# A fused attention and maxout kernel on one core: another table of order, engines and slots for the same 1542 nodes

## The chip, the cores and the metric

The kernel runs on one core of one Trainium2 chip, as one launch. The metric is device time in microseconds, taken as the median of several executions. The profile is of one further execution, and all durations here come from its trace.

## The reference

For each of 8 batches and 8 heads (576 tokens, head size 64) there is a linear attention with a feature map, and behind it one feed-forward layer that takes the larger of three products:

```python
def phi(x):                                   # w_phi: 64 x 128
    proj = np.einsum('bhsd,df->bhsf', x, w_phi)
    proj = proj - np.max(np.abs(proj), axis=-1, keepdims=True)
    return np.concatenate([np.exp(proj), np.exp(-proj)], axis=-1)
q_p, k_p = phi(q), phi(k)
kv = np.einsum('bhsf,bhsd->bhfd', k_p, v);  z = np.sum(k_p, axis=2)
attn = np.einsum('bhsf,bhfd->bhsd', q_p, kv) / (np.einsum('bhsf,bhf->bhs', q_p, z)[..., None] + 1e-06)
x = attn.transpose(0, 2, 1, 3).reshape(4608, 512)
h = np.maximum(np.maximum(x @ w1, x @ w2), x @ w3)    # 512 x 768 each
out = h @ w_out                                       # 768 x 512
```

## The kernel before, in words

**Units and chunks.** The attention is cut into 16 units of four heads (two units make one batch), the feed-forward layer into 9 chunks of 512 tokens: the first 512 tokens of each batch, and one chunk of the last 64 tokens of all batches. The program first writes down 1542 nodes in a list. A node is a small piece of work of one engine: its instructions, the nodes it depends on, the buffers it uses, and a guess of its cost. Nothing is issued while they are written down.

**The nodes of a unit u**, by the names that the code gives them (lines are those of the profile of before):

- loads: `L` (main part of q and of k, 512 tokens of each head), `Lt` (q or k of the last 64 tokens, called tails here, for two units at once, as two transfers), `Lv` and `Lw` (the same of v). Units 0 to 3 load the main parts of q and k on POOL's queue with a cast to bf16 (L474); unit 0's k comes in two halves on SP's queue (L461) and is cast by `C` (L466). Everything else is loaded from SP's queue (L373, L378). `C` on POOL (L504) casts tails, and for units 4 to 15 the main parts too.
- `T` transposes q and k: for units 0 to 3 on PE (L517) with `Tc` copying out (L520), from unit 4 on as a DMA transpose on SP (L530).
- `G` projects q and k (L557, L552); `r` takes the largest magnitude (DVE, L576); `ek` the exponentials of k (ACT, L570); `E` the factors that undo the shift on the side of v (ACT, L613).
- `va` multiplies v with these factors on POOL (L618 for the main part, L633 for the tails); `vd` copies the factors beside them (L628, L642).
- `K` multiplies features of k with v (PE, L682, L685), 18 matmuls a node, two nodes a unit; `kv` copies out (L689).
- `M` projects q with its shift (L653 to L657), `eq` is its exponential (L665), `N` the numerator and denominator (L703), `x` the division (L709, L710), `X` the transposition back (PE L723 for units 0 to 5, a DMA transpose later) and `Xc` its copy (L726). From unit 4 on `mT` and `V` send the shift of q through a small DMA (L588, L592).

**The nodes of the weights**: `W` loads one weight matrix with a cast on POOL's queue (L434, 768 KB of bf16 each); `wt`, `we`, `wm`, `mo` form w1 @ w_out (L843 to L861); `wd` forms w2 - w1 and w3 - w1 on POOL and DVE (L831). **The nodes of a chunk**: `up` and `up2` (PE, L756), `t1` and `h` (L764, L766, L762), `down` (L784 and L789), `osb` (L797), `store` (L804).

**What sets the order.** A table, `PLAN`, written out as a string (line 91 of before). Each word has the node's number, a letter for its engine (T for PE, D for DVE, A for ACT, G for POOL, S for SP), the slots of the buffers whose first user it is, and a start in microseconds as the search that made the table believed it. `plan` reads the table:

```python
n.eng, n.start = {"T": "PE", "D": "DVE", "A": "ACT", "G": "POOL", "S": "SP"}[what[at]], float(start)
n.end = n.start + n.costs[n.eng] + LATENCY[n.eng]
for b in n.bufs:
    if b.index is None:
        b.index = int(next(slots), 36)
```

`fill` then puts products of a constant tile, whose result nobody reads (`idler`, L889), into the stretches in which the table leaves PE without work, and sorts everything by its start; the kernel issues the nodes in that order. Engines take their own instructions strictly in that order. So the starts matter in two ways only: as an order on each engine, and as the places of idlers. What an instruction waits for at run time comes from its data and its buffers.

**Three kinds of waits that the steps need.** The raw tiles of q tails and k tails have one buffer each, so the tails of units 2 and 3 can't be loaded before POOL has cast those of units 0 and 1. The bf16 tile of q and k (`qk_bf`) has three slots, so unit 3's loads wait until unit 0's transposes are done. SP issues one transfer after another: one that has to wait holds back all behind it.

Of the kernel before, what the change touches and what calls it, by code (L numbers as in the profile page):

```python
# [105 lines left out]
191D@36.4 200D@37.0 243G@28.8 247G@29.6 132G@29.9 129G@30.9 134G@31.9 128G@32.2 133G@33.2 152T61@35.0 154T2@35.7
155A@36.5 203A@36.9 153A@37.3 1161T5@36.3 1145G@34.2 1162A@37.8 188A@38.3 196D@37.7 204D@38.3 78T20@37.6 68T0@37.9
79D0@38.6 69A@38.8 194A@39.3 187D@39.2 158T61@38.3 156T5@38.7 159D1@39.8 157D0@40.4 162T4@39.0 160T2@39.4 163D1@41.1
161D0@41.7 202A@39.8 206A0@40.1 184A@40.4 173S@33.2 221T11@39.9 224T7@40.4 212T6@40.6 174S@33.8 316S0@37.3 318S0@39.7
253T3@41.0 254D1@42.3 317S@42.0 387S@43.4 249T5@41.3 82T4@41.8 222A@40.9 70A@41.4 84T0@42.3 1163T2@42.6 80T3@43.9  # L110
83D1@42.5 85D0@43.1 225A@41.8 226A@42.3 223A@42.7 213A@43.2 214A@43.8 250D@43.8 245D@44.4 164T7@44.2 88T4@44.5
315S@46.1 89A@45.1 81D1@44.5 1147G@37.5 1164D@45.1 215T1@44.8 388S@47.8 86T0@45.3 166T6@45.6 165D@45.7 87D@46.2
216A@45.7 167A@46.2 255T10532411@45.9 246S@49.5 218T7@46.5 273T0@47.0 1149G@39.6 1148G@41.7 257A@46.9 275A@47.5
217A@47.8 274A@48.3 256A@48.6 1152D@46.7 262D@47.3 220A@49.1 219A@49.8 209A0@50.2 1175T6@47.2 1176D1@48.3 1173T2@48.1
1179T1@48.9 1171T6@49.8 210G0@44.7 208G@45.9 211G@47.8 207G@48.3 227T71@50.7 1174A@50.4 1172A@50.9 321G1@51.8
322G@53.0 229T2@51.3 230A@52.2 259D@49.3 1180D@50.1 251T3@51.9 1189T1@52.5 277D@50.7 258D@51.0 276D@51.6 1151D@52.0
252D@52.7 1150D@53.3 228A@52.6 264T6502@53.5 272D@54.3 1183T7@54.1 392G2@54.1 391G@54.3 390G@55.3 393G@56.3
1177T3@55.1 267D@54.9 271D@55.5 270A@55.1 269A@55.7 1178A@56.2 1184D@56.1 235T60@55.9 236D0@56.8 268D@57.4 263D@58.0
290T00@56.3 296T2@56.7 291A@57.0 284T3@57.0 286A@57.6 297A@58.1 298A@58.6 1190D@58.6 1191T7@57.4 265A@59.0 285A@59.4
292A@59.9 278A1@60.4 1192D@59.2 1169T6@58.3 323S0@54.2 1187T2@59.1 260A@60.7 266A@61.2 261A@61.6 281A1@62.1 1188D@60.3  # L120
237T1@60.0 231T7@60.3 293T3@60.6 233T0@61.1 295A@62.3 294A@62.9 1181T2@61.4 1193T5@62.3 238D1@60.9 232D0@61.5
1170D@62.1 234D1@62.7 458S0@57.1 459S@57.7 461S0@60.3 324T01174600@63.1 283A1@63.4 1182D@63.3 327D@64.0 342T0@63.7
1167G@56.6 280G@60.8 325A@64.0 282G@62.7 279G@63.9 1185T3@64.0 287T2@64.9 329A@64.5 288A@65.6 346D@64.6 1186D@65.2
394S2@61.6 1197T1@65.3 460S@64.5 299T30@66.2 300A@67.1 289A@67.5 1194T@66.8 328D@65.8 332D@66.4 345D@67.0 344A@68.0
319S0@65.1 343A@68.5 326A@68.8 331D@67.3 305T31@68.1 303T4@68.5 301T2@68.8 302A@69.6 330A@70.0 306D0@68.7 304D1@69.3
1195D0@69.9 1198T@69.4 1199A1@70.9 532G0@65.8 528S@66.7 320S@68.4 527S@71.1 464G1@66.1 465G@71.8 333T0734@70.7
337D@71.5 336D@72.1 340D@72.7 466S1@73.1 334A@72.3 339A@72.8 241T2@71.3 242A@73.3 309T6@71.7 307T5@72.0 308D0@73.3
310D1@74.0 1205T1@72.3 1206T@73.2 395T10032511@74.5 335A@73.9 1201T7@75.1 347T6@76.0 341D@74.6 350A0@75.3 338A@75.6
353G0@75.7 533G@76.0 531G@76.3 351G@77.3 530G@79.1 352G@80.1 401A@76.1 400A@76.7 402D@75.3 398D@75.9 313T2@76.1
311T4@76.4 239T0@76.7 348D0@76.5 1202T@77.0 240A@77.3 1207A2@77.9 1203A3@78.6 314D@76.7 403D@77.4 312D@78.0 397A@79.2  # L130
404T6205@78.3 413T4@78.9 407D@79.1 411D@79.7 399D@80.4 416D@81.0 410A@79.7 406A@80.2 355A0@80.6 409A@80.9 412D@81.5
1211T1@79.2 408D@82.2 1217T7@80.1 1215T6@80.9 1227T0@81.8 1212A0@81.4 396A@81.9 405A@82.9 1216D@82.8 418T1@82.7
1213T5@82.7 349S@76.9 389S@77.6 596S0@80.3 600S1@81.5 356T31@83.6 1209T6@83.8 1228D@83.5 419D1@84.1 417D@84.3
1214D@84.7 1210D@85.3 1218D@85.9 421A1@84.8 1208S@82.8 595S@83.4 420S@84.5 357A@85.1 358A@85.7 365T2@84.7 368T0@84.9
1223T1@85.0 424A1@86.2 354G@82.0 665S0@85.2 597S@85.8 1196S@86.4 370A@86.4 414A@86.7 1219T5@85.9 359T6@86.8 369A@87.0
360A@87.4 371T31@87.0 373T7@87.6 362T0@88.2 372D@87.9 1224D@88.3 1220D@88.9 669G2@84.8 664S@87.0 367A@87.9 361A@88.3
366A@88.8 1225T3@88.5 377T61@89.3 415A@89.3 1226D@89.6 436T10@89.7 425G1@85.2 1221T2@89.9 374D@90.2 378D0@90.6
364A@89.7 363A@90.3 375T5@90.7 381T4@91.1 376D1@91.3 382D0@91.9 439T3@91.4 379T7@91.5 430T0@91.8 1231T6@92.0
427T5@92.9 380D1@92.6 1222D@93.2 1229T4@93.1 1230D@94.3 1232D@94.9 433T7@94.0 438A@90.8 437A@91.4 441A@91.9 431A@92.3
383T1@94.2 428A@93.4 429A@94.0 422G@86.5 423G@88.4 426G@90.2 442T20@94.5 440A@94.5 434A@94.8 435A@95.5 432A@96.0  # L140
444T5@95.2 443D@95.5 445D@96.0 385T3@95.8 384D@96.4 386A@96.5 467T01462700@96.1 475D@96.9 471D@97.5 472A@97.7
# [4 lines left out]
491A0@104.6 477A@104.9 478A@105.5 670G@95.5 601G1@95.8 602G@96.9 668G@98.0 1238T@104.3 493A0@106.0 535T10510311@105.6
456T4@106.2 454T2@106.6 537A@106.4 457A@106.9 455A@107.6 603S2@98.1 1204S@102.8 540A@108.2 492S@105.0 1241T6@106.9
1239D1@105.8 538D@106.5 542D@107.1 544T7540@107.8 551D@108.6 547D@109.3 543D@109.9 548D@110.5 553T2@108.4 549A@108.7
550A@109.3 555A@109.8 536A@110.2 554A@110.7 541A@111.0 556D@111.1 552D@111.5 557D@112.1 539D@112.4 1242T@108.7
# [771 lines left out]
```

## Time and profile before

| | us |
|---|---|
| median of three timed executions | 297.06 (296.61 to 297.08) |
| span of the profiled execution, first to last instruction | 295.1 |
| PE busy in the span | 281.6 |
| DVE, ACT, POOL busy | 214.3, 196.3, 138.1 |
| idlers on PE | 37 products, 12.2 busy |
| mean granted PE clock | 0.998 |

The profiled execution is one of its own; its record is the span, and the timed median is 1.96 us longer than that span, because a timed execution also has what lies ahead of the first and behind the last instruction. Matmuls are pipelined: a 128x512 one is shown as busy for 379 ns, while the next starts 216 ns after it. So shares of busy time on PE overstate its work, and the distance between starts is the better measure.

### The profile page before, as it was taken

To read this page: it belongs to the slowest core of one execution; us is meant where nothing else is said; L and a number is where in the kernel's file an instruction comes from. 1 tells how busy PE (TensorE), PEld (TensorE's weight loads), DVE (VectorE), ACT (ScalarE), POOL (GpSimd) and SP (SyncE) were. 2 spreads that over 40 slices of the span, in tenths; PEclk is the share of its full clock that TensorE was granted. 3 is DMA by queue.
4 is the path that set the end of the run, shared out by engine and by line. 5 is a ranking of instruction groups with operands and counts; after the bars stand their busy time and mean duration, and the time that the engine had idled before them with its cause. 6 is when DMAs were issued, how large, how long until landed. Compare 5 with 4: busy or idle time off the path is not lost.

```text
span 295.1 us, 7535 instructions
## 1 busy us (share of the span) xinstructions
PE 281.6 (95%) x2973; PEld 161.5 (55%) x3015; DVE 214.3 (73%) x453; ACT 196.3 (67%) x457; POOL 138.1 (47%) x172
## 2 busy tenths in 40 slices
PE   8699999999999999999999999999999999999994
PEld 3356676556556556556556555655555564444442
DVE  5793798987878988888879776889697365061541
ACT  2499888587878599979879788867954870300300
POOL 4487995672773464943982369009072500000000
PEclk9999999999999999999999999999999999999999
DMA  6999998799379979997979779935392034300306
GB/s 134 190 196 224 229 221 286 167 234 226 99 182 328 209 203 318 230 230 167 285 165 189 220 204 244 189 102 117 90 209 64 2 83 116 142 2 0 142 8 134
DMA packets 87879, 50.02 MB, mean 170 GB/s; under 512 B 56100, under 2 KB 83364, under 8 KB 87844
## 3 DMA queue, kind: packets, MB, share of 16 engines
q1 hardware_dynamic: 81684, 44.50, 61.2%
q0 software_dynamic: 6080, 4.98, 11.0%
q8 instruction: 23, 0.38, 0.5%
q14 instruction: 12, 0.10, 0.1%
q10 hardware_dynamic: 80, 0.07, 0.1%
HBM read 34.67 MB, written 9.44 MB: 149 GB/s over the span
## 4 chain that ended last, share of the span: by engine, by line
PE 79%; DVE 9%; ACT 4%; POOL 3%; DMA 2%; issue 2%; POOLq 0%; ACTq 0%; DVEq 0%
PE ups L756 27%; PE ops L789 15%; PE ops L784 11%; PE psn L703 6%; PE kvps L682 5%; PE psq L557 4%; PE psm L653 4%; DVE mk L576 2%; DMA qk_bf<-in_q_dram 2%; ACT Ek L570 2%; DVE mqp L576 2%; DVE x_sb L710 1%; POOL vab L618 1%; PE pxT L723 1%; DVE w_bf L831 1%
## 5 line engine op out<-in xcount | busy, mean ns | idle before, releaser
L756 PE MATMUL ups<-xT,w_bf 128*128 128x512 bf16 x412 | 100.4, 379 | 2.2 <-DVE mqp L576 0.8
L665 ACT ACTIVATE Eq<-psm 128x512 bf16<-128x512 f32 (+1 forms) x160 | 79.6, 579 | 8.8 <-PE psm L653 7.3
L570 ACT ACTIVATE Ek<-psk 128x512 bf16<-128x512 f32 x128 | 70.8, 607 | 16.1 <-DVE mk L576 8.7
L618 POOL TENSOR_TENSOR vab<-v_raw,em 128x1024 bf16<-128x1024 f32 (+1 forms) x36 | 61.6, 1715 | 21.2 <-ACT em L613 20.1
L756 PEld LDWEIGHTS <-w_bf 128*128 128x128 bf16 x432 | 40.7, 98 | 45.3 <-issue 1.0
L576 DVE TENSOR_REDUCE mqp<-psq 128x4 bf16<-128x512 f32 (+1 forms) x80 | 47.7, 629 | 7.5 <-PE psk L557 4.4
L789 PE MATMUL ops<-wout_bf,hT 128*128 128x512 bf16 (+1 forms) x211 | 49.5, 373 | 0.6 <-issue 0.2
L762 DVE TENSOR_TENSOR hT<-hT,ups 128x512 bf16<-128x512 bf16 x54 | 36.0, 683 | 17.4 <-PE ups L756 9.1
L576 DVE TENSOR_REDUCE mk<-psk 128x4 f32<-128x512 f32 x64 | 42.2, 680 | 1.1 <-PE psk L557 0.7
L710 DVE TENSOR_TENSOR x_sb<-psn,rden 128x320 bf16<-128x320 f32 x64 | 31.5, 492 | 2.2
L789 PEld LDWEIGHTS <-hT 128*128 128x128 bf16 x222 | 21.1, 98 | 21.7
L797 ACT COPY osb<-ops 128x512 f32<-128x512 f32 (+1 forms) x20 | 11.5, 581 | 31.3 <-PE ops L789 23.6
L764 ACT ACTIVATE hT<-ups 128x512 bf16<-128x512 f32 x27 | 16.4, 617 | 21.5 <-PE ups L756 21.5
L703 PEld LDWEIGHTS <-Eq 128*128 128x128 bf16 x640 | 24.6, 97 | 6.8
L703 PE MATMUL psn<-kv_sb,Eq 128*128 128x65 bf16 x640 | 26.1, 194 | 0.1
L633 POOL TENSOR_TENSOR vtl<-v_raw,em 64x256 bf16<-64x256 f32 x32 | 19.7, 615 | 13.2 <-ACT em L613 10.2
L766 DVE TENSOR_SCALAR hT<-ups 128x512 bf16<-128x512 f32 x27 | 18.1, 683 | 10.6 <-PE ups L756 10.6
L784 PE MATMUL ops<-xT 128*128 128x512 bf16 x89 | 24.1, 379 | 0.4
L682 PEld LDWEIGHTS <-Ek 128*128 128x128 bf16 x512 | 21.6, 98 | 4.5 <-DVE mqp L576 0.5
L682 PE MATMUL kvps<-vab,Ek 128*128 128x65 bf16 x512 | 22.8, 194 | 0.5 <-DVE mqp L576 0.2
L504 POOL CAST qk_bf<-q_raw 128x128 bf16<-128x128 f32 (+2 forms) x22 | 16.8, 773 | 11.6 <-DMA q_raw<-in_q_dram 11.3
L797 DVE COPY osb<-ops 128x512 f32<-128x512 f32 (+1 forms) x17 | 11.4, 671 | 13.7 <-PE ops L789 13.6
(80 smaller groups left out, 333.5 us busy)
## 6 DMA issues: line engine op xcount, KB each, us to landing
v_raw<-in_v_dram SPq DMA_DIRECT2D x16, 512.0 KB, 6.8
out_dram<-osb SPq DMA_DIRECT2D x32, 256.0 KB, 2.9
k_raw<-in_k_dram SPq DMA_DIRECT2D x12, 512.0 KB, 5.6
q_raw<-in_q_dram SPq DMA_DIRECT2D x12, 512.0 KB
w_bf<-in_moe_w_dram POOLq DMA_DIRECT2D x3, 768.0 KB, 8.3
k_raw<-in_k_dram SPq DMA_DIRECT2D x16, 64.0 KB, 4.5
q_raw<-in_q_dram SPq DMA_DIRECT2D x16, 64.0 KB, 6.4
v_raw<-in_v_dram SPq DMA_DIRECT2D x16, 64.0 KB, 4.3
```

The lines of the kernel that those rows point to most:

```text
L570: nc.scalar.activation(Ek[s]()[:, t0:t0 + n, :], of(1), EXP, scale=1.0 - 2.0 * s)
L576: nc.vector.tensor_reduce((mq, mk)[c]()[:, t0:t0 + n], of(c), AXX, ALU.max, apply_absolute_value=True)
L618: (nc.vector if n_.eng == "DVE" else nc.gpsimd).tensor_tensor(vab()[:, g, t0:t1, 0:D], raw_part(u, 2, t0, t1), em()[:, g, t0:t1].unsqueeze ...
L665: nc.scalar.activation(Eqb()[s][:, cols], psm()[:, 0:n * P], EXP, scale=1.0 - 2.0 * s)
L682: nc.tensor.matmul(kvps()[:, ab, g, :], lhsT=Ek[g]()[:, t, :], rhs=vab()[:, g, t, :], start=(g + ab + c == 0), stop=False)
L703: nc.tensor.matmul(psn()[:, c, :], lhsT=Eqb()[g][:, t0:t0 + P], rhs=kv()[:, pr, ab, g, :], start=(g == 0), stop=(g == 1))
L710: nc.vector.tensor_tensor(x_sb()[:, pr, :, ab, :], psn()[:, :, 0:D], rden().to_broadcast([P, 5, D]), ALU.mult)
L756: nc.tensor.matmul(ups(), lhsT=w_bf[i + 1][:, ct, j * P:(j + 1) * P], rhs=tokens_of(ct), start=(ct == 0), stop=(ct == CT - 1))
L762: nc.vector.tensor_tensor(hT()[:, j, :], hT()[:, j, :], ups(), ALU.max)
L784: nc.tensor.matmul(ops_()[:, 0:width], lhsT=tile_of(ct, tt), rhs=line_w[c_i > MOVE][:, ct, cols], start=(ct == 0), stop=False)
L789: nc.tensor.matmul(ops_()[:, 0:width], lhsT=hT()[:, j, tt * P:(tt + 1) * P], rhs=wout_bf[:, j, cols], start=False, stop=(j == JT - 1))
L797: copy_on[n_.eng](part()[:, 0:width], ops_()[:, 0:width])
```

## The change

Only the table changes: the 156 lines of `PLAN` become 154. No instruction, cost, dependency or buffer count is touched. Of the 1542 nodes, 88 go to another engine (of the first evacuations of the maxout, `t1`, 16 go from DVE to ACT and 6 back; of `osb` 10 each way; of `vd` 17, of `kv` 13, of `Xc` 6, of `mT` 5, and a few more), 547 get other slots, and the order on every engine is another from the first microseconds on. The words now stand in the order of their starts. PE has 24 idlers instead of 37. Line numbers after the table are lower by 2.

The head of the table, and the last line of each:

```diff
 PLAN = """
-9S0@0.7 4S@1.3 11S@2.5 13S@3.1 8S0@4.4 15S0@5.6 14S@6.9 6G0@0.5 0G@1.4 1G@2.1 7G@2.6 90G1@3.4 17G@9.3 91G@9.6 12A@6.8
-2D0@0.5 3D@0.8 10D@5.3 18T1@5.9 5D@5.7 19D0@6.7 29T002300@7.5 94G@10.4 95G@10.7 20T4@7.8 24T56@8.3 32D@8.0 21D@8.7
-33D@9.3 27D@9.9 16G@10.9 1143G@11.1 34T71@9.4 39T24@9.7 22T5@11.3 38D@10.5 28D@11.1 30A@10.0 31A@10.7 40A@11.2
...
-1532S@292.7 1536S@293.9
+9S0@0.4 6G0@0.4 2D0@0.4 3D@0.8 4S@1.0 7G@1.2 0G@2.1 11S@2.2 1G@2.8 8S0@2.8 91G1@3.3 10A@3.5 13S@4.1 90G@4.2 5D@4.4
+18T1@4.4 170G2@5.0 19D0@5.1 12A@5.3 15S0@5.3 168G@5.8 24T002300@5.9 92D@5.9 29T45@6.1 27D@6.4 25A@6.4 20T6@6.4
+1143G@6.7 30A@6.8 28D@7.0 16G@7.5 21D@7.6 26A@7.8 17G@7.8 95G@8.1 32D@8.2 22T7@8.2 31A@8.2 94G@8.3 34T12@8.4 244G0@8.6
+169S0@8.7 100T6@8.8 23D@8.8 35A@8.9 39T34@9.0 37D@9.1 44T7@9.3 243G@9.4 41A@9.5 42D@9.7 36A@10.0 171S0@10.0 47D@10.3
+1146G@10.3 40A@10.4 33D@10.6 62T10@10.8 45A@10.9 1144G@11.1 59T3@11.2 14S@11.2 38D@11.2 49A0@11.4 63A@11.6 68T5@11.6
...
+1537T0@282.9 1475A2@283.2 1538T@283.4 1476S@283.9 1539D0@284.3 1540S@284.8 1541A@284.8
 """
```

**What stands where in the first part**, read from the built programs' order on each queue:

| queue | before | after |
|---|---|---|
| SP | k halves and w_phi, k tails, q tails, v tails of units 0 and 1, `Lv` of unit 0 (node 14), k tails and q tails of units 2 and 3 (171, 169), `Lv` of unit 1 (93) | k halves and w_phi, q tails, k tails, v tails of units 0 and 1, q tails and k tails of units 2 and 3 (169, 171), then `Lv` of unit 0 (14) and of unit 1 (93) |
| POOL | q of unit 0, first half (6), the identity, second half (7), q of unit 1, casts of tails, k of unit 1 between them, W of w1 and w_out, `va` of unit 0, loads of unit 2 and k of unit 3, rest of `va` of unit 0, w2, casts of the tails of units 2 and 3, `va` of unit 1, w3, `wd` | both halves of q of unit 0, the identity, k and q of unit 1, k and q of unit 2, w1, the four casts of tails of units 0 and 1 (16, 17, 95, 94), k and q of unit 3, w_out, w2, w3, the four casts of tails of units 2 and 3 (247, 175, 176, 248), then all of `va` of unit 0 (57, 55, 54, 50, 51) and of unit 1 |
| PE | transposes of unit 0's main part, all four `G` of that part, then the transposes of unit 0's tails (22) | transposes of unit 0's main part, two `G`, then the transposes of unit 0's tails (22), then the other two `G` |
| PE, ahead of the first `K` of unit 0 | all `T` and `G` of units 0 and 1, 9 `M`, 3 `wt`, 35 idlers | the same `T` and `G`, all `T` of unit 2, one of unit 3, 6 `M`, 3 `wt`, 24 idlers |

The last store of before is issued on SP in two pieces; after, it is one piece on SP and one on ACT.

More of the change, by code (lines that the diff above doesn't have):

```diff
@@ L146 @@
[L146 to L149, printed above, removed]
-1251T4@110.0 1257T7@110.9 1269T3@111.8 735S0@105.7 734S@107.0 802S@107.6 546A@111.5 1243A3@112.0 545A@112.6
@@ new lines @@
+101D1@11.8 1145G@11.9 43D@12.0 46A@12.1 98T2@12.2 69A@12.4 96T6@12.6 48D@12.6 60A@12.9 247G@12.9 99D@13.0
+122T11411@13.2 175G@13.2 61A@13.6 97D@13.6 117T72@13.8 93S@13.9 70A@14.0 65T3@14.2 125D@14.2 53A@14.5 121D@14.6
+176G@14.8 64A@14.8 248G@15.0 177T6@15.1 120D@15.2 57G0@15.2 118A@15.3 179T5@15.5 126D@15.8 66A@15.8 107T17@16.1
+178D2@16.1 124A@16.3 58G@16.5 67A@16.6 111D@16.7 181T6@16.9 123A@17.1 180D@17.3 119A@17.5 102T34@17.6 109A@18.0
+182D@18.0 112T25@18.1 110D@18.2 52A0@18.4 71T6@18.4 108A@18.6 55G@18.6 116D@18.8 388S0@18.9 253T1@18.9 103A@19.1
@@ new lines @@
+755A@142.8 704T4@143.0 757D@143.2 1305T0@143.2 1280S@143.3 752A@143.4 753D@143.8 706A@143.9 736S@143.9 713T7@144.1
+1297T2@144.3 658D1@144.4 1302D@145.0 719T61@145.2 1298A@145.4 758D@145.7 721T1@145.8 714A@145.9 874S0@146.0
+1306D@146.3 707T5@146.4 715A@146.6 1303T2@146.6 722D@146.9 705A@147.1 720D@147.3 872S@147.5 827T00000@147.5
+767A0@147.5 764T7@147.7 1304D@147.8 708A@147.8 1307T1@147.8 941G1@148.0 765A0@148.3 756A@148.5 766S@148.8
+818T4627@148.8 1308D@148.9 828A@149.0 875G2@149.0 1309T3@149.3 709A@149.4 663S@149.5 825D@149.5 822D@150.1
@@ new lines @@
+936D1@198.7 1016A@199.3 1379T1@199.3 1034A@199.8 1021A@200.1 984T7@200.2 1037D@200.3 995T41@200.4 1380D@200.6
+992A@200.6 1355A1@200.9 913T0@201.1 1019D@201.2 993T3@201.3 1082S0@201.5 986A@201.5 996D@201.8 1024T6152@202.0
+985A@202.2 994D@202.2 987T4@202.6 914A@202.7 1032D@202.7 1391T3@202.8 915A@203.3 1031D@203.3 1369T7@203.6 988A@203.8
+1027D@203.9 1030A@204.3 981T0@204.5 1392D@204.5 1001T51@204.7 989A@204.8 931T6@205.1 1028D@205.2 1385T3@205.4
+1002D0@205.8 1041A0@205.9 982A@206.2 933T4@206.2 1043G0@206.3 932D1@206.4 1387T5@206.6 1029A@206.6 934D0@207.0
@@ new lines @@
+983A@207.1 1381T6@207.4 1026A@207.6 1388D@207.7 937S@207.8 1042G@208.2 1025A@208.3 1003T2@208.3 1386D@208.3
+997T4@208.6 1370A@208.8 999T0@208.9 1038T5@209.3 1393T1@209.3 1000D1@209.5 1490G@210.1 1382D@210.1 1368S@210.2
+1405T3@210.2 1045G0@210.5 1039D0@210.8 998D0@211.0 1040S@211.1 1083T00706500@211.2 1397T4@211.7 1086D@211.9
+1085A@211.9 1004D1@212.5 1084A@212.5 1394T@212.6 1089A@213.0 1087D@213.2 1005S@213.3 1090D@213.8 1406T@213.9
+1395A2@214.2 1092T7201@215.3 1407A0@215.5 1101T6@215.9 1099D@216.0 1098A@216.1 1398T@216.1 1088A@216.6 1100D@216.7
```

275 lines of the change are left out of this document (128 added, 147 removed).

## The prediction

> **What bounds the kernel now.** I read the shares and slices first, then the busy time by stretch, then the chain of waits, then single queues in the first 36 us.
>
> ```profile
> PE 281.6 (95%) x2973; PEld 161.5 (55%) x3015; DVE 214.3 (73%) x453; ACT 196.3 (67%) x457; POOL 138.1 (47%) x172
> ...
> 0.00:26.70 26.70, 21.80 (x241) 11.53 (x241) 18.59 (x45) 17.04 (x44) 16.17 (x32) 1.00 1.04 181
> 26.70:34.30 7.60, 7.30 (x119) 4.58 (x120) 3.37 (x8) 6.76 (x15) 7.48 (x13) 1.00 1.27 215
> 34.30:60.00 25.70, 24.45 (x340) 16.44 (x346) 24.25 (x51) 19.93 (x47) 18.55 (x17) 1.00 0.92 229
> 60.00:250.00 190.00, 187.57 (x2081) 109.75 (x2113) 152.55 (x326) 145.86 (x343) 95.92 (x112) 1.00 0.75 181
> 250.00:291.00 41.00, 40.50 (x196) 19.18 (x196) 15.54 (x24) 6.57 (x12) 0.00 (x0) 1.00 0.21 66
> ```
>
> The columns after the stretch and its length are busy us of PE, weight loads, DVE, ACT and POOL, then the granted PE clock, the DMA share and GB/s. From 34.3 us on PE is idle for 25.70 - 24.45 + 190.00 - 187.57 + 0.50 = 4.2 us in all. A new order can save at most that there. The time lies in the first 34.3 us: by distances between starts (a node of 16 transposes 0.6 us, a group of eight `G` products 0.23, `M` 0.44, `K` 0.64, `wt` 0.45, `wm` 1.30) PE does some 16.1 us of real work in them, of which 9.8 before the first `K`. The rest are idlers and waits. The chain of waits says for what:
>
> ```profile
> 3.32 5.79 DMA qk_bf<-in_q_dram
> ...
> 19.19 3.10 ACT Ek L570 x6
> ...
> 26.70 0.43 PE kvps L682 x8
> ```
>
> First loads, then ACT at 3.10 / 6 = 0.52 us an exponential, end the waits; at 26.70 the first `K` starts, and the first of unit 1 starts at 34.33. DMA is the other full resource there: its share is 1.04 and 1.27 in the two stretches, while it is 0.75 later.
>
> **A yardstick.** PE has almost the same work ahead of these two points in both orders. Ahead of unit 0's first `K`: 9.8 us before, 10.1 us after (six `M` for nine, four more nodes of transposes). Ahead of unit 1's first `K`: 16.1 us before, 15.5 us after (four `N`, four `M` and more for `wm` and `G` of unit 2). So PE's end moves by what unit 1's `K` moves, plus 0.6 us that is left to do after it, less what idle time goes later. The table's starts are what its search believed; no time is taken from them.
>
> **The steps to that point, from queue rows of before.** Issues on SP, then POOL:
>
> ```profile
> 3.10 1.31 SPq L378 DMA_DIRECT2D k_raw<-in_k_dram  x2
> 4.45 1.28 SPq L378 DMA_DIRECT2D q_raw<-in_q_dram  x2
> 5.77 1.27 SPq L378 DMA_DIRECT2D v_raw<-in_v_dram  x2
> 7.09 0.60 SPq L373 DMA_DIRECT2D v_raw<-in_v_dram  x1
> 12.21 1.27 SPq L378 DMA_DIRECT2D k_raw<-in_k_dram  x2
> 13.58 1.79 SPq L378 DMA_DIRECT2D q_raw<-in_q_dram  x2
> 21.25 0.37 SPq L373 DMA_DIRECT2D v_raw<-in_v_dram  x1
> ```
>
> ```profile
> 9.46 0.29 POOL L504 CAST qk_bf<-k_raw 128x128 bf16<-128x128 f32 x1 [4.57 <-DMA k_raw<-in_k_dram]
> ...
> 11.64 0.30 POOL L504 CAST qk_bf<-q_raw 128x128 bf16<-128x128 f32 x1 [0.97 <-DMA q_raw<-in_q_dram]
> ...
> 12.47 0.30 PE L517 MATMUL tps<-ident,qk_bf 128*64 128x128 bf16 x4 [0.51 <-POOL qk_bf L504]
> ```
>
> 1. *First transposes.* Their load is POOL's first instruction in both; it lands at 5.75, PE starts at 5.79. No change.
> 2. *Second half of q.* It is issued at 2.1 instead of 3.32, so it lands some 1.2 us or more before 9.11. A gain, if something behind it can use it.
> 3. *Tails of unit 0.* The pairs of q and k tails change places but keep their times, so POOL has cast both at 12 us again (9.46 and 11.64 above), and PE transposes them at 12.4 again. But now these four transposes stand ahead of half the `G` of the main part, which ran at 10.6 to 11.2 before. An added wait: PE's queue stands from 8.6 to 12.4, and behind it two `G`, six exponentials on ACT, and every `M` of unit 0. The gain of step 2 is used up here.
> 4. *Tails of units 2 and 3.* They wait for those casts as before (12.21), and take until 14.9 at 0.62 to 0.65 an issue. Same time.
> 5. *v of unit 0.* Its load stood ahead of them (7.09), and now stands behind them: 14.9, later by 7.8. `Lv` of unit 1 follows at 15.5, earlier by 5.7.
> 6. *POOL.* After its first casts it issues five big loads until about 17, then stands for the tails of units 2 and 3, and only then starts `va` of unit 0, which before ran from 15.89. So `K` of unit 0 waits for two landings in a row. How long these take is the disputed number. DMA by queue, from 3 to 12 us and from 12 to 24:
>
> ```profile
> q1 hardware_dynamic: 2488, 1.15, 56.3%
> q0 software_dynamic: 1107, 0.54, 50.5%
> ```
>
> ```profile
> q0 software_dynamic: 1913, 1.87, 96.1%
> q1 hardware_dynamic: 1181, 0.35, 18.2%
> ```
>
> Columns: packets, MB, share of 16 engines. While POOL's queue (q0) held weights, SP's queue (q1) moved 0.35 MB in 12 us, though tails were waiting in it. After, POOL's queue holds two more loads of unit 2 and all four weights from 5 us on, and SP's holds 0.77 MB (tails and `Lv` of unit 0) from 12.3 on. Landings measured under such load: tails 4.5 and 6.4 us (first pairs), 7.2 (units 2 and 3, next to weights), up to 9.3 for the last of four by the trace's semaphore records, which puts the last at 23.56; `Lv` of unit 1 7.3, which is 5.0 behind that tail. So the last tail (issued at 14.2) lands between 20.6 and 23.5; I take 22, as 7 to 8 is the row with weights beside it. `Lv` (14.9) lands between 22.2 (7.3 later) and 28.6 (5.0 behind the latest tail); I take 25.0. Then POOL needs four `va` at 1.04: `K` of unit 0 at 29.2 (26.6 to 32.8), and two of 0.62 and four of 1.04 more, with their gaps 5.4: `K` of unit 1 at **34.7** (32 to 38).
>
> **Other parts.** 88 nodes change engine: `t1` costs 617 ns on ACT, 683 on DVE, so ten more on ACT move about 6 to 7 us from an engine that is 73% busy to one at 67%. Both are covered by PE, 98.7% busy from 60 to 250; nothing. If that cover went, the late one would be ACT, by 6 us over 230. The 13 idlers that go (0.23 us apart) only stood in waits: nothing. Slots alone cost nothing unless a wait follows; I count that with the next item.
>
> *Loads of later units.* The table leaves less room: unit 8's k has 3.9 us from issue to cast where before had 12.4, unit 10's k 3.9 for 10.3, unit 12's v 3.8 for 8.1. Median landings are 5.6 (k) and 6.8 (v). Three such places, each late by 2 to 3, with slack behind some: between 0 (PE is late itself) and 5; I take +1.5. *Idle time after 34.3*: 4.2 us; none to all of it goes; I take -1.0, since most lies in pieces of 0.2. *The end*: SP's last issues run 0.6 apart, and one now goes to ACT: -0.6 (-1.2 to 0).
>
> **Sum**, against the profiled span of 295.1: unit 1's `K` +0.4 (-2.4 to +3.8), work left +0.6, later loads +1.5, idle -1.0, end -0.6: +0.9, a span of 296.0. With the 1.96 us between the span and the median of the timed runs: **298.0**.
>
> **Rivals.**
>
> - *A, the loads land when the new order wants them.* For it: the same DMA work is asked for sooner, and ACT, idle for 4.0 us before 11.2, would start at 7.6. Against it: rows of step 6. ACT then sets the pace: 30 exponentials of units 0 and 1, six more and small ones, at 0.52 some 21.5 us from 7.6, so unit 1's `K` at 29.1: -5.2 + 0.6 - 1.0 - 0.6, **290.9**. It needs tails that land within 4.5 us everywhere. Chance 0.14. Between A and the forecast, 293.5 to 296.5: 0.16.
> - *B, POOL's queue holds v back.* If the last tail lands later than 23.5 and v 5 us behind it, unit 1's `K` comes at 38.1: +3.8 + 0.6 + 1.5 - 0.6, **302.4**. For it: 18.2% and 0.35 MB above. It decides from the point where v of unit 0 lands after 28. Chance 0.15.
> - [...] Chance 0.15. [...]
> - *The change does not do what it says*: excluded, as the order on every queue differs and the instructions are the same but for idlers.
>
> **How the numbers follow.** Forecast (296.5 to 300) 0.40, A 0.14, between 0.16, B 0.15, C 0.15. A measurement of this kernel tells about 0.2% (0.6 us) from no change: under 296.5 is faster, over 297.7 slower. Faster: 0.14 + 0.16 and a little of the forecast, 0.32. Same: the forecast's lowest third, 0.14. Slower: 0.54. The range leaves out the better half of A and the worse third of B: 292 to 303. Both signs hold much; the forecast's own range is 296.5 to 300.
>
> **What would show it.** Step 3: PE's four tail transposes of unit 0 at 12.4, with the two `G` behind. Step 5: v of unit 0 issued at 14.9. Step 6: `va` of unit 0 not before 22, unit 0's `K` at 29, unit 1's at 34.7. [...] I am wrong if tails land in 4 us beside weights: then unit 0's `K` comes before 25.

## The result, and the profile after

The changed kernel takes **299.88 us** (298.25 to 300.79), the kernel before 297.06 in the same rounds: a ratio of 1.009, with a 95% interval of 1.0064 to 1.0117. Timed again later it took 298.74, a ratio of 1.0047 (1.0018 to 1.0076). So the new table costs some 1.4 to 2.7 us. The profiled execution has a span of 298.8 us (295.1 before). The two profiled executions of the changed kernel took 300.62 and 299.67 us, 0.7 and 0.9 above their medians, so what the profiles show as lost is a little more than the median loses. Line numbers are two lower than before: the va at L618 is now L616.

| us | before | changed | changed, second profile |
|---|---|---|---|
| first `K` of unit 0 | 26.70 | 29.37 | 28.54 |
| first `K` of unit 1 | 34.33 | 35.38 | 34.54 |
| end of PE | 290.66 | 294.74 | 293.79 |
| from unit 1's `K` to the end of PE | 256.33 | 259.36 | 259.25 |
| from there to the end of the span | 4.42 | 4.08 | 4.07 |

Three parts can be read from this table: at most 1.05 us of the loss arises before unit 1's `K`, about 3.0 arises behind it, and 0.35 comes back at the end. 0.8 of the 3.0 is work that now stands behind that `K` instead of ahead of it. Busy time by stretch, with the columns as in the prediction:

```profile
0.00:29.37 29.37, 23.23 (x256) 13.18 (x257) 20.40 (x48) 18.27 (x45) 16.27 (x34) 0.94 1.13 196
29.37:35.38 6.01, 5.56 (x129) 4.89 (x129) 3.29 (x11) 4.56 (x12) 5.37 (x7) 1.00 1.14 241
...
60.00:250.00 190.00, 187.23 (x2154) 110.17 (x2152) 148.82 (x320) 149.41 (x349) 97.70 (x120) 1.00 0.69 173
```

The first stretch, up to unit 0's `K`, is 2.7 us longer, and for the first time a clock below 1.00 (0.94) stands in it. SP's queue shows v of unit 0 behind the tails of units 2 and 3 (before, it was issued ahead of them, at 7.09):

```profile
13.43 1.26 SPq L376 DMA_DIRECT2D q_raw<-in_q_dram  x2
14.80 1.25 SPq L376 DMA_DIRECT2D k_raw<-in_k_dram  x2
16.09 1.55 SPq L371 DMA_DIRECT2D v_raw<-in_v_dram  x2
```

POOL's queue shows what follows from that (in brackets: how long POOL stood ahead of the piece, and what ended it):

```profile
12.63 0.53 POOL L502 CAST qk_bf<-k_raw 128x128 bf16<-128x128 f32 x2 [4.32 <-DMA k_raw<-in_k_dram]
...
21.50 0.53 POOL L502 CAST qk_bf<-q_raw 128x128 bf16<-128x128 f32 x2 [3.78 <-DMA q_raw<-in_q_dram]
23.67 0.53 POOL L502 CAST qk_bf<-k_raw 128x128 bf16<-128x128 f32 x2 [1.64 <-DMA k_raw<-in_k_dram]
...
27.27 4.05 POOL L616 TENSOR_TENSOR vab<-v_raw,em 128x512 bf16<-128x512 f32 x4 [1.34 <-DMA v_raw<-in_v_dram]
```

POOL stands three times for a landing of tails, and once more for v, before the four main `va` of unit 0 start at 27.27. In the kernel before, their first three ran from 15.89, ahead of the casts:

```profile
15.89 3.05 POOL L618 TENSOR_TENSOR vab<-v_raw,em 128x512 bf16<-128x512 f32 x3 [1.62 <-ACT em L613]
```

In the changed kernel unit 0's `K` starts when the second of them is done:

```profile
29.37 0.42 PE L680 MATMUL kvps<-vab,Ek 128*128 128x65 bf16 x8 [1.40 <-POOL vab L616]
```

PE's waits, summed over the span (us, times, longest):

```profile
PE tps L515 <- POOL qk_bf L502: 2.8, 2, 1.5
PE kvps L680 <- POOL vab L616: 2.2, 3, 1.4
PE psm L651 <- DMA qkT<-mT: 2.1, 1, 2.1
...
PE psq L550 <- DMA qkT<-qk_bf: 0.6, 1, 0.6
```

The first two lie ahead of unit 1's `K` or around it: tail transposes at 12.98 and 24.02, `K` at 29.37. The last two lie later: `M` of unit 6 at 108 waits for its transfer `V`, and `G` of unit 13 at 190 waits for its transpose `T`. By distances between starts these two are 2.3 and 0.8 us; in the second profile 1.6 and 1.6. The kernel before has no wait over 0.7 us behind its first `K`.

### The profile page after: what moved, and what is told of

It is laid out like the page before. It is cut to its first block, busy times and chain, and to the rows that moved or that the text cites. A ratio compares the mean times of both kernels' runs of the same rounds, so it can differ in the third digit from the quotient of the medians.

```text
span 298.8 us, 7548 instructions
## 1 busy us (share of the span) xinstructions
PE 284.6 (95%) x3002; PEld 162.8 (54%) x3002; DVE 209.1 (70%) x444; ACT 200.4 (67%) x463; POOL 137.6 (46%) x175
## 3 DMA queue, kind: packets, MB, share of 16 engines
q0 software_dynamic: 6080, 4.98, 10.5%
## 4 chain that ended last, share of the span: by engine, by line
PE 78%; DMA 13%; DVE 4%; SPq 1%; issue 1%; POOL 1%; POOLq 0%; DVEq 0%
PE ups L754 29%; PE ops L787 15%; PE ops L782 10%; PE psn L701 6%; DMA v_raw<-in_v_dram 5%; PE psq L555 5%; PE kvps L680 4%; PE psm L651 4%; DMA qkT<-qk_bf 3%; DMA k_raw<-in_k_dram 2%; DMA qkT<-mT 2%; PE pm L855 1%; DVE mk L574 1%; PE pxT L721 1%; PE kvps L683 1%
## 5 line engine op out<-in xcount | busy, mean ns | idle before, releaser
L754 PE MATMUL ups<-xT,w_bf 128*128 128x512 bf16 x432 | 102.5, 379 | 0.4 <-DVE hT L764 0.4
L663 ACT ACTIVATE Eq<-psm 128x512 bf16<-128x512 f32 (+1 forms) x160 | 82.6, 576 | 10.0 <-PE psm L651 8.0
L568 ACT ACTIVATE Ek<-psk 128x512 bf16<-128x512 f32 x128 | 72.4, 608 | 17.8 <-PE psk L555 12.8
L616 POOL TENSOR_TENSOR vab<-v_raw,em 128x1024 bf16<-128x1024 f32 (+1 forms) x36 | 61.1, 1714 | 41.1 <-ACT em L611 20.2
L574 DVE TENSOR_REDUCE mqp<-psq 128x4 bf16<-128x512 f32 (+1 forms) x80 | 48.9, 630 | 9.0 <-PE psk L555 5.0
L787 PE MATMUL ops<-wout_bf,hT 128*128 128x512 bf16 (+1 forms) x222 | 51.2, 373 | 0.0
L574 DVE TENSOR_REDUCE mk<-psk 128x4 f32<-128x512 f32 x64 | 42.9, 683 | 2.2 <-PE psk L555 1.2
L762 ACT ACTIVATE hT<-ups 128x512 bf16<-128x512 f32 x37 | 21.5, 602 | 32.3 <-PE ups L754 32.0
L795 DVE COPY osb<-ops 128x512 f32<-128x512 f32 (+1 forms) x17 | 11.4, 673 | 26.4 <-PE ops L787 23.8
L701 PE MATMUL psn<-kv_sb,Eq 128*128 128x65 bf16 x640 | 26.9, 194 | 0.0
L502 POOL CAST qk_bf<-k_raw 128x128 bf16<-128x128 f32 (+2 forms) x22 | 15.7, 729 | 17.8 <-DMA k_raw<-in_k_dram 16.8
L795 ACT COPY osb<-ops 128x512 f32<-128x512 f32 (+1 forms) x20 | 11.6, 588 | 17.2 <-PE ops L787 16.9
L502 POOL CAST qk_bf<-q_raw 128x128 bf16<-128x128 f32 (+2 forms) x22 | 15.8, 728 | 14.9 <-DMA q_raw<-in_q_dram 8.7
## 6 DMA issues: line engine op xcount, KB each, us to landing
out_dram<-osb SPq DMA_DIRECT2D x32, 256.0 KB, 2.7
w_bf<-in_moe_w_dram POOLq DMA_DIRECT2D x3, 768.0 KB, 22.2
```

The source lines that it names most:

```text
L502: copy_on[n_.eng](dst, raw_part(u, c, t0, t1))
L568: nc.scalar.activation(Ek[s]()[:, t0:t0 + n, :], of(1), EXP, scale=1.0 - 2.0 * s)
L574: nc.vector.tensor_reduce((mq, mk)[c]()[:, t0:t0 + n], of(c), AXX, ALU.max, apply_absolute_value=True)
L616: (nc.vector if n_.eng == "DVE" else nc.gpsimd).tensor_tensor(vab()[:, g, t0:t1, 0:D], raw_part(u, 2, t0, t1), em()[:, g, t0:t1].unsqueeze ...
L663: nc.scalar.activation(Eqb()[s][:, cols], psm()[:, 0:n * P], EXP, scale=1.0 - 2.0 * s)
L701: nc.tensor.matmul(psn()[:, c, :], lhsT=Eqb()[g][:, t0:t0 + P], rhs=kv()[:, pr, ab, g, :], start=(g == 0), stop=(g == 1))
```

## Experiments

The **load and POOL theory**: v of unit 0, late on SP and then behind two casts on POOL, makes the first `K` late. Rivals: the order of PE (its tail transposes, early in PE's queue, wait for casts); the clock; the **later-order theory**: two transfers with too little room make the loss behind 37 us. Edits are moves of nodes in the table, shown as words of it (node, engine letter, slots, start); only the order that the starts give counts. The ratio is to the kernel before as timed in the same rounds, and compares best between runs.

| run | median us | ratio to before (95%) | `K` of unit 0, of unit 1 | unit 1's `K` to end of PE |
|---|---|---|---|---|
| changed kernel | 299.88 | 1.009 (1.0064 to 1.0117) | 29.37, 35.38 | 259.4 |
| v early on SP | 299.34 | 1.009 (1.0057 to 1.0124) | 29.84, 35.23 | 258.6 |
| v early on SP and POOL | 297.0 | 1.0001 (0.9975 to 1.0027) | 26.11, 32.11 | 257.6 |
| before, v late on SP | 306.59 | 1.0307 (1.0286 to 1.0329) | 28.37, 45.30 | 256.7 |
| v and M of unit 6 | 301.45 | 1.0149 (1.0117 to 1.0182) | 29.15, 35.16 | 260.2 |
| six idlers | 297.84 | 1.0034 (1.0011 to 1.0058) | 28.40, 34.40 | 256.9 |
| tails later on PE | 300.5 | 1.0145 (1.0114 to 1.0177) | 28.47, 35.06 | 258.9 |
| later room | 297.57 | 1.0054 (1.0026 to 1.0082) | 28.51, 34.52 | 256.0 |
| all sets | 296.2 | 0.9993 (0.997 to 1.0017) | 25.97, 33.18 | 257.6 |
| changed again | 298.74 | 1.0047 (1.0018 to 1.0076) | 28.54, 34.54 | 259.3 |
| later room, idlers | 297.8 | 1.0023 (1.0000 to 1.0047) | 28.94, 34.94 | 256.4 |
| all sets, idlers | 294.5 | 0.9914 (0.9881 to 0.9946) | 25.54, 32.40 | 255.9 |
| va of unit 1 first | 294.35 | 0.9918 (0.9888 to 0.9947) | 25.88, 31.25 | 258.4 |

**v early on SP.** One load alone goes back to its old place in SP's queue:

```diff
-15S0@5.3 ... 169S0@8.7 171S0@10.0 14S@11.2
+15S0@5.3 14S@7 ... 169S0@8.7 171S0@10.0
```

> The changed order, with one load moved on SP: v of unit 0 is issued right behind the tails of unit 0/1 (7.1 us, as in the kernel before) and so ahead of the tails of units 2/3. Load theory (SP's place of this load makes the first K late): va of unit 0 need not wait for it, but still stands on POOL behind the casts of those tails, which end near 24; the 1.3 us that POOL waited for the load go: first K of unit 0 28 instead of 29.4, first K of unit 1 34 instead of 35.4, time 1.0 to 1.4 below the changed kernel. POOL-queue theory (the casts in front of va hold it, the load alone does nothing): 0 to 0.5 below. Later-order theory (the loss arises behind 37 us): K of unit 1 earlier, but time less than 0.5 below.

Nothing was gained: 299.34, with unit 0's `K` at 29.84. POOL's queue in this run:

```profile
22.13 0.53 POOL L502 CAST qk_bf<-q_raw 128x128 bf16<-128x128 f32 x2 [5.71 <-DMA q_raw<-in_q_dram]
24.32 0.54 POOL L502 CAST qk_bf<-k_raw 128x128 bf16<-128x128 f32 x2 [1.65 <-DMA k_raw<-in_k_dram]
...
26.67 4.05 POOL L616 TENSOR_TENSOR vab<-v_raw,em 128x512 bf16<-128x512 f32 x4
```

The stand for v is gone from the last line, but the tails landed 0.6 us later, with v ahead of them, and the casts still stand in front of `va`. The load by itself is not the bound, which is the POOL-queue reading. But unit 0's `K` did not start with the second `va` here (26.67 + 2.1 = 28.8, by the distance that the other profiles of this order show): PE came to it 1.1 us later, without a wait. Behind its own waits for the casts it had run at half clock from 25.7 to 29.1:

```profile
25.00:30.00 5.00, 5.00 (x59) 3.84 (x59) 4.66 (x9) 3.73 (x13) 4.77 (x8) 0.66 1.20 232
```

With a full clock that `K` would have come near 28.8, still not at the 28 of the load theory.

**v early on SP and POOL.** Both `Lv` go ahead of the tails on SP, the `va` of unit 0 ahead of the casts on POOL, and the tail transposes of units 2 and 3, which would now hold PE, behind unit 0's `K`:

```diff
-14S@11.2 93S@13.9 50G@20.6 51G@21.6 57G0@15.2 58G@16.5 55G@18.6 54G@19.6 247G@12.9 175G@13.2 176G@14.8
+14S@7 93S@7.1 50G0@12 51G@12.1 57G0@14.6 58G@14.65 55G@14.7 54G@14.75 247G@14.8 175G@14.82 176G@14.84
-181T6@16.9 182D@18.0 253T1@18.9 254D0@19.4
+181T6@23.85 253T1@23.86 182D@23.95 254D0@23.96
```

> The changed order with v of units 0 and 1 issued at 7 us on SP, the four va and the tail's va of unit 0 on POOL ahead of the casts of units 2/3's tails, and the transposes of those tails on PE behind unit 0's K. Load and POOL-queue theories: POOL starts va at 17.7 when its loads are issued, the last va of unit 0 ends near 24.5, first K of unit 0 at 24 to 25 (29.4 before), first K of unit 1 at 30.5 to 32 (35.4), time 2.5 to 4 below the changed kernel, 296 to 297.5, if what follows keeps up. Clock theory (the 3.4 us at half clock from 13.9 delay everything that follows): K of unit 0 no earlier than 28, time at most 0.5 below. Later-order theory: K earlier as told, but waits grow behind it and the time falls by less than 1.

It fell by 2.9 us to 297.0, the time of the kernel before (by 1.7 against the changed kernel's second timing). POOL now takes v first:

```profile
18.45 2.05 POOL L616 TENSOR_TENSOR vab<-v_raw,em 128x512 bf16<-128x512 f32 x2 [1.61 <-DMA v_raw<-in_v_dram]
...
24.97 0.53 POOL L502 CAST qk_bf<-q_raw 128x128 bf16<-128x128 f32 x2 [0.62 <-DMA q_raw<-in_q_dram]
27.66 0.54 POOL L502 CAST qk_bf<-k_raw 128x128 bf16<-128x128 f32 x2 [2.16 <-DMA k_raw<-in_k_dram]
```

Unit 0's `K` came 3.3 us earlier than in the changed kernel's first profile and 2.4 earlier than in its second, and unit 1's by the same. Unit 0's is 1 us later than expected; 0.6 of it is a wait of PE for ACT's exponentials at 25.5. Unit 1's is where it was expected, with no wait of PE over 0.4 us between the two. The orders of SP, POOL and PE were moved together here; the order of POOL alone was not run. The clock was at half here too (12.5 to 15.9), so the clock theory's "no earlier than 28" is refuted.

**Before, v late on SP.** The other way round: in the kernel before, that one load goes behind the tails.

```diff
-14S@6.9 ... 171S0@11.1 ... 169S0@14.5
+171S0@11.1 ... 169S0@14.5 14S@15
```

> The kernel before, with one load moved on SP alone: v of unit 0 behind the tails of units 2/3, issued at 15.4 instead of 7.1. Load theory: POOL, which takes va at 15.9 in the kernel before, waits for the landing (18 to 24) with its loads of q and k behind it; first K of unit 0 at 28.8 to 35 instead of 26.7, K of unit 1 2 to 7 late, time 1.5 to 6 above the kernel before. Rival (va has slack at that place, the order of PE sets the start): within 0.5 of the kernel before.

It cost 9.6 us, more than the theory's 1.5 to 6. POOL, then PE:

```profile
27.27 3.05 POOL L618 TENSOR_TENSOR vab<-v_raw,em 128x512 bf16<-128x512 f32 x3 [13.53 <-DMA v_raw<-in_v_dram]
```

```profile
28.37 0.42 PE L682 MATMUL kvps<-vab,Ek 128*128 128x65 bf16 x8 [2.32 <-POOL vab L618]
35.47 0.27 PE L685 MATMUL kvps<-vtl,Ek 128*128 128x130 bf16 x1 [6.68 <-POOL vtl L642]
```

Issued at 14.14, v is there only at 27.27, 13.1 us later. POOL stands for 13.5 us with all of `va` of unit 0, three loads and a copy (`vd`) behind it, and PE waits a second time, 6.7 us, for that copy: a POOL queue with all of it behind one late load. In these pauses the clock fell too, to half from 30.7 to 40.9, and PE worked in it from 35.5 on: of the loss, up to 2.7 us (half of 5.4) is the clock's, an estimate. Unit 1's `K` is 11 us late, and behind it nothing more is lost (256.7). The changed kernel has its casts and big loads on POOL ahead of `va`, and so paid less.

**v and M of unit 6.** In the changed kernel, the two loads of v of unit 6 ahead of a store on SP, a load of k behind `V`, and three `M` behind a down product and two `X` on PE (one moved `M` takes another PSUM bank):

```diff
-1236S@91.6 463S1@92.2 462S@93.4 802S0@94.1 492S@95.9
+462S1@91.5 463S@91.55 1236S@91.6 492S@95.9 802S0@95.95
-508T70@99.2 499T0@99.4 511T2@100.9
+508T50@102.05 499T0@102.06 511T2@102.07
```

> The changed order with the place of its longest later PE wait eased (2.3 us at 108, M of unit 6 waiting for the transfer mT to qkT): on SP the two loads of v of unit 6 stand ahead of a store, a load of k stands behind the transfer, and on PE the three M stand behind a down product and two X. Later-order theory: v lands 2 us earlier, K of unit 6 at 110.6 instead of 112.4, time 1 to 2 below the changed kernel. Rival (a wait there is made good by slack behind it, or comes back at the next transfer): the wait goes and the time is within 0.4.

The wait for `V` went and the time did not fall: 301.45. As the rival says, the waits moved: `X` waited 1.0 for an `eq` that the bank change put in front of it, `K` of unit 6 waited 0.9 for its `va`, and unit 13's `G` 2.1. Why the time is 1.6 above the changed kernel is not settled; the profile accounts for 0.6 of it at the end of PE.

**Six idlers.** In the changed kernel, six more products into the pause in front of unit 0's tail transposes:

```diff
-    return [fn for _, fn in sorted(todo, key=lambda x: x[0])]
+    todo += [(8.15 + 0.001 * i, make(0)) for i in range(6)]; return [fn for _, fn in sorted(todo, key=lambda x: x[0])]
```

> The changed kernel with six more idlers on PE in front of the tail transposes of unit 0, so that PE works through the pause of 11.5 to 13 (they compute nothing that is used). Clock theory (the half clock from 13.9 to 17.3 after that pause makes the first K late): clock 1.00 there, K of unit 0 some 1.5 us earlier, time 1 to 1.5 below the changed kernel. Load and POOL theory: clock 1.00 there too, but K of unit 0 still at 29 to 29.8, since its last va ends on POOL at 29.3; time within 0.6 of the changed kernel.

The clock was 1.00 from 9 to 19, and `K` of units 0 and 1 came at 28.40 and 34.40. Against the first profile of the changed kernel that is 1.0 earlier; against the second, 0.14. The time fell by 2.0 (first) or 0.9 (second), more than the POOL theory had, but not through `K`: behind unit 1's `K`, unit 13's wait was absent in this profile. Against the second timing it is not clear of noise (ratios 1.0034 and 1.0047, with overlapping intervals). The clock did fall in this profile, from 24.4 to 27.8, behind PE's two waits for the tail transposes of units 2 and 3.

**Tails later on PE.** Only the PE part of the second experiment:

```diff
-181T6@16.9 182D@18.0 253T1@18.9 254D0@19.4
+181T6@23.85 253T1@23.86 182D@23.95 254D0@23.96
```

> The changed kernel with one part of the second experiment alone: on PE the tail transposes of units 2/3 stand behind K of unit 0; SP and POOL as they are. PE-order theory (PE's wait of 1.5 us at 22.5 for the casts of those tails makes K late): K of unit 0 at 28 and time 1 to 1.5 below the changed kernel. Load and POOL theory: the wait at 22.5 goes and stands in front of unit 0's K, which stays at 29 to 29.6; K of unit 1, whose em then comes earlier, 0 to 1 us earlier; time 0 to 0.8 below.

As the POOL theory says: the wait went in front of `K` (1.8 us), and the time did not fall (300.5). `K` came at 28.47, earlier than the 29 to 29.6 of that theory, because `va` itself started at 26.4; in the changed kernel's second profile it came at 28.54 with no edit at all. The order of PE alone is not the cause.

**Later room.** Three transfers into stretches where SP stood idle; the first 40 us stay:

```diff
-603S1@87.3 ... 463S1@92.2 462S@93.4 ... 834S@162.5 ... 945S2@169.8
+462S1@86.9 463S@86.95 603S1@87.3 ... 945S2@162 834S@162.5
```

> The changed kernel with three transfers moved on SP into stretches where SP stands idle: the two loads of v of unit 6 ahead of a transpose (93 instead of 101 to 103), so that the transfer mT to qkT of unit 6 has fewer loads ahead, and the transpose of unit 13 ahead of a transfer (169.5 instead of 180.6), where six loads stood ahead of it. The first 40 us are as in the changed kernel. Later-order theory: the waits at 108 (2.3 us) and at 189 (0.8 us, 2.2 in two other runs) go, and the time falls by 2 to 3.5. Rival (waits move on to the next late transfer, as in the run with v of unit 6 alone): time falls by less than 0.8.

Both waits went. Among the longest waits of this run, down to 0.6 us in all, only these two are PE's, and both lie in the first 23 us:

```profile
PE tps L515 <- POOL qk_bf L502: 5.0, 3, 1.7
PE idler L887 <- DVE idle L425: 1.0, 1, 1.0
```

From unit 1's `K` to the end of PE it is 256.0 us, 3.3 less than in both profiles of the changed kernel, and as in the kernel before. So in the profiles the loss behind 37 us is these two transfers. The time fell by less: 2.3 against the first timing of the changed kernel, 1.2 against the second. The profiled execution was the fastest of its kernel (296.40, the median 297.57), and the ratio to the kernel before, 1.0054, is not below the 1.0047 of the changed kernel's second timing. That the later room gains time by itself is thus not shown.

**All sets.** The second experiment, the later room, and the four `G` of unit 0 ahead of its tail transposes:

```diff
-32D@8.2 22T7@8.2 34T12@8.4 39T34@9.0 37D@9.1 42D@9.7
+32D@8 34T12@8.12 39T34@8.16 22T7@8.2 37D@8.5 42D@8.55
```

> Both sets together: v and va of unit 0 early on SP and POOL with the tail transposes of units 2/3 behind K (as in the second experiment), the three later transfers moved into SP's idle stretches, and on PE the four G of unit 0 ahead of its tail transposes, for which PE waited 1.5 to 2.8 us. If the losses add: 2.9 us (second experiment) and 2 to 3 (later room) below the changed kernel, 294 to 295, below the kernel before by 2 to 3. If the later waits move on: 296 to 297, as the kernel before.

296.2, inside the second expectation (the later waits move on) and not to be told from the kernel before (0.9993, 0.997 to 1.0017). The losses do not add up as the first expectation had it.

**Changed again.** The changed kernel without any edit, beside the three runs that follow.

> The changed kernel itself, unaltered, beside the three below: how much its first K, its clock and its later waits differ from one execution to the next. Expected 299 to 300.5 us; a low clock after the pause before unit 0's tail transposes, as in 4 of 6 profiles with that pause so far (not in those of v of unit 6 and of later room); first K of unit 1 between 34.5 and 35.5; waits of 1.3 to 2.3 for unit 6 and of 0.8 to 2.3 for unit 13.

298.74 us; the numbers stand in the table. Its pause before the tail transposes of unit 0 was 1.8 us, and the clock stayed at 1.00 behind it. It fell later, from 23.5 to 26.9, behind two waits of 1.9 and 1.7 us for the tail transposes of units 2 and 3:

```profile
23.00:26.00 3.00, 2.90 (x29) 1.60 (x30) 1.87 (x5) 1.06 (x4) 1.87 (x6) 0.58 1.18 246
```

Unit 1's `K` is 0.2 us later than before instead of 1.05.

**Later room, idlers** (both edits as above).

> The two parts that gained most for their size, together: six idlers in the pause (2.0 below the changed kernel alone) and the three transfers moved on SP (2.3 below alone). If idlers act by the clock, a thing of their own: the gains add, 295.6 to 296.4. If both came to the end by the same way, the waits at 108 and 189 (idlers shift the order in which transfers meet): no more than the transfers alone, 297.2 to 297.9.

No gain over the later room alone (297.8 and 297.57). This does not test the clock: the profile of the later room had no drop behind the pause that the idlers fill, and both profiles have one behind the tail transposes of units 2 and 3 (23.4 to 26.8 and 23.8 to 27.2).

**All sets, idlers** (both edits as above).

> The run with all sets and six idlers in the pause in front of unit 0's tail transposes. There va no longer stands at the end of a long POOL queue, unit 0's K waited 0.6 us for ACT, and PE had half the clock from about 12 to 15.5. Clock theory: 1 to 1.5 below that run (7 runs of it at a clock of 0.999 or more had a mean of 295.7, 5 at 0.994 had 297.4): 294.7 to 295.4. If POOL's va of unit 1 sets the pace: within 0.5 of 296.2.

**294.5 us**, 1.7 below the run without idlers and 2.4 below the kernel before: a ratio of 0.9914, 0.9881 to 0.9946. The stretch from 13 to 15 us, first without and then with the six idlers (the clock is the third number from the end):

```profile
13.00:15.00 2.00, 2.00 (x10) 0.89 (x7) 0.81 (x2) 0.36 (x1) 2.00 (x3) 0.50 1.24 252
```

```profile
13.00:15.00 2.00, 2.00 (x16) 0.99 (x17) 1.49 (x4) 1.72 (x4) 1.15 (x2) 1.00 1.25 252
```

ACT did 0.36 us of work in these 2 us at half clock, and 1.72 at full. Unit 1's `K` came 0.8 earlier; the rest of the gain lies behind it, where two waits of 0.7 and 1.0 us were absent. The timed executions say how much is the clock's: without the idlers, seven of the twelve kept a mean clock of 0.999 or more and took 295.7 on average, the five at 0.994 took 297.4. Had all kept it, their mean would be 0.7 us lower; the other 1 us of the gain is not explained by the clock.

**va of unit 1 first.** As the last, and the casts of the k tails behind unit 1's `va`, with what reads them:

```diff
-176G@14.84 248G@15.0 388S0@18.9 181T6@23.85 253T1@23.86 318S@26.6 201T00200@26.9
+176G@26.92 248G@26.94 388S0@27 318S@27.05 181T6@30.45 253T1@30.47 201T00200@30.58
```

> As the run before it, and on POOL the casts of the k tails of units 2/3 behind the va of unit 1 too, their transposes and the G that reads them on PE behind unit 1's K, two loads of units 4/5 on SP behind those casts. In the run with all sets K of unit 1 came at 33.2, behind a cast that waited for a k tail until 29.2. Load and POOL theory: K of unit 1 at 29.5 to 31.5, time 1 to 2 below that run, 294 to 295.2, below the kernel before. Rival (PE's own work ahead of that K, and later loads, are the bound by then): within 0.5 of the run with all sets and idlers.

Unit 1's `K` came at 31.25, 1.15 earlier, and the time stayed (294.35). The rival holds as far as the time goes. In the profile, PE's own work stands ahead of that `K`, and a wait of 1.3 us for a transpose at 99 takes the gain; but this execution (295.56) is 1.2 us above the median, so what takes it in the others is not shown.

## Why the prediction was right or wrong, point by point

The forecast was 298.0 with its own range of 296.5 to 300. Its mechanism, a first `K` held by v behind the tails on SP and POOL, is what the runs show; two terms of the sum were sized wrong. With what was measured the sum is +1.05 (unit 1's `K`), +0.8 (work left), +3.1 (later loads), -0.9 (idle), -0.35 (the end): +3.7 on the span, where +0.9 was forecast. The second profile has +0.2 for the first of them, and +2.8 in all.

- *What bounds the kernel.* Right: the first 34 us, and the yardstick held. In cost units of the table the work left behind unit 1's `K` grew by 0.8 us (0.6 forecast).
- *Step 1*: 5.83 for 5.79, right. *Step 2*: q's second half landed at 7.06 instead of 9.11, but PE's transposes of it stayed at 9.19, because PE was busy up to then: it was still at the slow pace of its first microseconds (idlers 0.43 us apart until after 7, in the kernel before only until 3.9) and worked on idlers and the first 16 products of `G`. The cast of k's second half on ACT, the other thing that they need, was done at 8.1. The gain was not used, as said, though for another reason.
- *Step 3*: right in its place. One transpose ran at 11.23 and three at 12.98, for 12.4 forecast; two `G` stood behind. PE's queue stood for 1.5 us, not from 8.6 to 12.4, since its own work lasted until 11.5.
- *Steps 4 and 5*: the tails were issued at 13.43 to 16.05 and v at 16.09, for 12.3 to 14.9 and 14.9. They hang on the cast of the k tail, which came at 12.63 in this profile. In the profiles of the same first stretch it came between 10.7 and 12.6, and all that follows moved with it: this is most of the spread of unit 0's `K`, 28.4 to 29.4.
- *Step 6*: the last tail was cast at 23.67 (22 forecast) and v taken at 27.27 (25.0). Unit 0's `K` at 29.37 agrees with 29.2 only because two errors cancel: v landed 11 us after its issue, longer than any row I had used, and that `K` needs two `va`, not four. That agreement is luck. (Two sums of this step are off by a little: 22.2 and four `va` give 26.4, not 26.6, and 29.2 + 5.4 is 34.6, not 34.7.) Unit 1's `K`: 35.38, and 34.54 in the second profile, for **34.7**. The term was +0.4 and measured +1.05 and +0.2.
- *Later loads*: the mis-sized term. +1.5 forecast, 3.1 us in both profiles by PE's waits. It named loads of k and v of units 8, 10 and 12; none of them kept PE waiting. The places were a small transfer (`V` of unit 6), issued at 104.79 behind a store and four load transfers of the 4 us before it, and landed after 5.4 us, and a transpose (`T` of unit 13) behind eight load transfers, 9.9 us from issue to landing. *Idle time elsewhere* -1.0: some -0.9 is left over when the rows above are added up (3.0 = 0.8 + 3.1 - 0.9). *The end* -0.6: -0.35.
- *Engines changed*: DVE's busy time fell by 5.2 us and ACT's rose by 4.1; PE covers it, as said.
- *Rival B* was near: it decides when v lands after 28, and v landed at about 27.2. *Rival A*: out; no tail landed in 4.5 us beside weights. But where va does not stand behind those casts, the order gets close to what A hoped for: 294.5.
- *Rival C*, a fall of the PE clock: it came, at another place than unit 0's `K`. The pause in front of that `K` was 1.4 us, and the clock did not fall behind it. In the first profile it fell behind the pause at 11.5, of 1.5 us; in the second, behind the waits at 19 to 23, as shown above:

```profile
11.00:13.00 2.00, 0.49 (x5) 0.13 (x3) 0.58 (x1) 0.34 (x1) 0.37 (x2) 1.00 1.37 185
13.00:14.00 1.00, 1.00 (x21) 0.71 (x23) 0.65 (x2) 0.33 (x1) 0.50 (x3) 0.90 1.34 200
14.00:17.00 3.00, 3.00 (x19) 1.58 (x15) 2.92 (x7) 2.31 (x7) 3.00 (x5) 0.50 1.19 211
```

  In the changed kernel no cost of it can be measured: its 8 executions with a mean clock of 0.991 or more took 299.2 us on average, the 13 with a lower one 299.3. In both profiles unit 0's `K` started 2.1 us behind the first `va`, whatever the clock had done. With v first on POOL, filling the pause was worth 1.7 us, of which some 0.7 by the clock. Of the eight profiles with a pause of PE of 1.3 to 2.6 us between 9 and 13, five show a fall of the clock within 0.9 us of its end and three show none there (runs in the last section).

**What stays open.** Whether the later room or the idlers, each by itself, gain time: the ratios of the changed kernel again (1.0047), of each of the two (1.0054, 1.0034) and of both (1.0023) have overlapping intervals. Where some 1 us of the gain of the idlers with all sets comes from. And why the runs with v and M of unit 6 and with tails later on PE were slower than the changed kernel. A part can be chance: unit 13's wait lay between 0 and 2.3 us in profiles with the same queue order there, and the changed kernel's own two medians differ by 1.1.

## What to carry to other kernels

When a table reorders an in-order machine, follow the loads that feed the first large product through every queue that they pass, the issuing one and that of the engine which casts: one load moved on SP cost 9.6 us in one order (part of it through the clock) and was worth nothing in the other, where the consumer's queue held it anyway. Give small transfers that PE waits for room by the traffic in front of them, not by their own size: `V` of unit 6 needed 5.4 us, the transpose of unit 13 9.9. Here a pause was worth filling only where the work behind it was not held by something else: with v first on POOL six idlers gained 1.7 us, in the changed kernel alone nothing that is clear of noise.

## What the runs showed of the hardware

- Half clock came in stretches of 3.4 us, or of two or three times that. Of the 11 drops to half inside the kernels nine lasted 3.4 us: 13.8 to 17.2 in the changed kernel, 12.0 to 15.4 (v early on SP), 12.5 to 15.9 (v early on SP and POOL), 11.9 to 15.3 (all sets), and five that began between 23.4 and 25.7. One lasted 6.8 us (11.4 to 18.2, tails later on PE) and one 10.2 (30.7 to 40.9, before with v late). In the profiles of the kernel before and of the changed one the changes of the clock also lie a whole number of such stretches apart. Before: a rise at 3.80 (idlers start 0.43 us apart ahead of it, 0.22 behind it) and a fall at 293.93, 85 times 3.413 us later. Changed: a rise at 10.38 (idlers 0.43 us apart at 7.2, 0.22 from 10.5 on), the fall and rise at 13.80 and 17.21, and a fall at 297.10, 82 times 3.413 us after the last of these.
- The length of a pause alone did not tell whether half clock came. It came with pauses of 1.3 us (all sets), 1.5 (changed kernel), 2.0 (v early on SP) and 2.6 (v early on SP and POOL, tails later on PE). It did not come with those of 1.6 or 1.7 us (later room), 1.8 (changed kernel, second profile) and 2.5 (v and M of unit 6): there the clock was 1.00 up to 17. Cut the profiles of the kernel before and of the changed one into steps of 3.413 us at the changes of their clocks: from the first rise to 285 us only the step with the most idle PE was followed by half clock, 10.38 to 13.80 in the changed kernel, with 1.51 us idle. The next ones, 1.43 us (before, 7.21 to 10.62), 1.42 and 1.40 (changed, from 20.62 and 27.45), were not. More than that on the cause is not shown. None of the four runs with idlers in the pause at 11 showed a drop behind it; two of them, six idlers and later room with idlers, had one at 24.
- Beside POOL's queue with weights, v of 512 KB took 11 us from SP (issued at 16.09) and 13.1 us (at 14.14, before with v late), where the row of before had 7.3. In these three orders the same kind of load has three landing times; a row of one order is no price for another.
